# Block 0's later query norm at n = 26 of group 0 instead of n = 6, in a transformer block on Trainium2

## The chip, the cores and the metric

One NeuronCore of a Trainium2 chip. The metric is the device time of one execution in microseconds; the kernel before took 1415.19 us (median of 3 runs, 1414.46 to 1415.21).

## The reference

A pre-norm block in float32 on x of 2048 rows and 512 columns: attention with 32 heads of 16 columns that share one key and one value head, then a gated feed-forward layer with 1792 hidden columns.

```python
q = (layernorm(x) @ wq), 32 heads of 16
k, v = layernorm(x) @ wk, layernorm(x) @ wv
o = softmax(q @ k.T / 4) @ v          # each head against all 2048 keys
h = x + o @ wo
out = h + (gelu(layernorm(h) @ w_gate) * (layernorm(h) @ w_up)) @ w_down
```

## The kernel before, in words

The rows are cut into four blocks of 512 (b = 0 to 3), the heads into eight groups of four. A **prologue** normalizes x, projects the keys and values of all rows, and the queries of block 0. Then comes one long run of **scores**, numbered n. For each block, group and 128 keys (`kc`) there are two scores, n even and odd, of two heads each: two matmuls into a PSUM tile `s`, and one exponential on ScalarE of 128x1024 numbers into `p` (`scores`, line 414). There are three such PSUM tiles, so the score n has to wait until ScalarE has read n - 3. Both n done, `weigh` (line 418) multiplies `p` with the values into `acc`. A group is 32 values of n, a block is 256. What the code calls a pair is one n.

Precision. Queries and keys are split into a high and a low part (`qh`, `ql`), which stand with a bound for the softmax as 50 rows for each head. They go through a DRAM tensor, `q_d`, from which `load_q` fetches a group's 50 rows (`qg`) one group ahead, on the sync engine's queue (SP). Two heads' rows lie at partitions 0 to 49, two at 64 to 113.

**The bound** needs a norm of each query. `project_q` (line 189) projects 128 query columns (8 heads) at a time, c = 0 to 3, from PSUM tiles `pq`, splits them, squares them into `qs`, and its inner function `norm` (line 260) sums the squares by head: one small matmul for each c against the selector `sel` into `pqn` (line 263), a copy to `qn` and its maximum on VectorE (lines 267, 268). `bound`, called two steps of the loop later, works four tiny operations and one of 32x512 on GpSimd (lines 273 to 290) and issues a transfer of the bounds to `q_d` (line 294). `load_q` of a group that the norm covers has to wait for that transfer. Block 0's queries are done as c = 0 alone (`q_first`, groups 0 and 1, in the prologue) and c = 1 to 3 (`q_rest`, groups 2 to 7).

**The queries of blocks 1 to 3** (`later_q`) are projected during block 0's scores, half the rows of PE at a time: one matmul of the projection (line 408, `pq`) runs beside one of the scores (line 410, `s`), on the two halves of the array. `qg_first`, the queries of group 0, therefore holds each head in both halves; the prologue's `first_q` fills one half for each head, `fill_first` (line 346) the other, by two transfers on GpSimd's queue (line 350). The order is set by hand: the loop at n < `lead` takes a string of kinds, "s" a plain score, "m" one beside a projection, from the table `MIXED`; the first mixed one is at n = `START` = 8. From then on `later_q` is asked for its next matmul; where it answers `REST`, a slot of two plain scores is run and behind them what the generator does next: the norm of the block before, at the first c of the next (line 232), or at the end of `later_q`. In that phase `psum1` has one bank, which `pq` and `pqn` use in turn.

At n = 2 the loop takes `q_rest` one step on, which splits c = 3 and writes it to `q_d`, and calls `fill_first`. At n = 6 it takes `q_rest` to its end: the three pqn matmuls for c = 1 to 3 stand on PE behind the score n = 5 and ahead of the first weighing. The generators for blocks 1 to 3 don't run their norm themselves but leave it in the list `norms`.

The order of PE, ScalarE and GpSimd is as the code is recorded throughout, and SP's and VectorE's too in this loop. GpSimd also splits the feed-forward weights during block 0 (`part_weights`: load on SP, cast, difference, store, lines 518 to 533).

Of the kernel before, what the change touches and what calls it, by code (L numbers as in the profile page):

```python
# [13 lines left out]
AF = mybir.ActivationFunctionType  # L14
# [40 lines left out]
def kernel(  # L55
# [12 lines left out]
    nc = tc.nc  # L68
# [83 lines left out]
    def attend(first):  # L152
        with ExitStack() as outer:
            with tc.manual_schedule(
                engines={mybir.EngineType.PE, mybir.EngineType.Pool, mybir.EngineType.Activation}
            ):
                run(outer, first)


    def run(outer, first):  # L160
# [28 lines left out]
        def project_q(b, cs, eng, col, whole=None):  # L189
            halves = whole is not None  # L190
# [3 lines left out]
            urgent = b == 0 and cs[0] == 0  # L194
# [102 lines left out]
                    after.append([2, bound])  # L297
                return qn, mm, m, factors

            if halves:  # L300
                norms.append(norm)
                return
            qn, mm, m, factors = norm()
            if urgent:
                yield 2
                factors()
                nc.scalar.activation(
                    m, qn, AF.Identity, bias=mm[:, 2:3], scale=mm[:, 1:2]
                )
                ms[b] = m  # L310
            else:
                yield 2


        after, squares, norms, pause = [], [], [], [0]
        ms = {}
        q_first = project_q(0, range(FIRST_Q), nc.scalar, 0)
        q_rest = project_q(0, range(FIRST_Q, DC), nc.scalar, NB)

        def later_q():  # L320

            for b in range(1, NB):
                yield from project_q(b, range(DC), nc.vector, b, ())
            yield REST
            yield REST
            norms.pop()()

        def age():
            for entry in after:
                entry[0] -= 1  # L330
            while after and after[0][0] <= 0:
                after.pop(0)[1]()
# [13 lines left out]
        def fill_first():  # L346

            view = q_d.rearrange("h r s -> r h s")
            for a in range(2):
                nc.gpsimd.dma_start(  # L350
                    qg_first[64 * a : 64 * a + KR, 1 - a :: 2, :].bitcast(F32),
                    view[:, 1 - a : 4 : 2, :T].bitcast(F32),
                )
# [71 lines left out]
        def take_out():  # L425
            for step in outs.pop(0):
                step()
# [151 lines left out]
        def load_wo(b):  # L579

            for j in range(DC // 2):
                w = db.tile([P, 2, 2, D], F32R, tag="w2", bufs=W2, name=f"wo_{b}_{j}")
                nc.sync.dma_start(
                    w.bitcast(F32),
                    wo_d[2 * j : 2 * j + 2].rearrange("c p i d -> p c i d").bitcast(F32),
                )
                wos[b, 2 * j], wos[b, 2 * j + 1] = w[:, 0], w[:, 1]
# [416 lines left out]
        def finish(n):  # L1004
            for _ in range(min(n, len(pend))):
                pb, pg, pkc, pp, pacc, _ = pend.pop(0)
                weigh(pacc, pp, pkc)
                if pkc == KC - 1:
                    evacuate(pb, pg, pacc)
# [17 lines left out]
        def score(n, beside=()):  # L1027

            nonlocal acc
            i, u = divmod(n, 2)  # L1030
            b, r = divmod(i, PER)
            g, kc = divmod(r, KC)
            if u == 0:
                if kc == 0:
                    cur["qg"] = qgs.pop((b, g))
                    acc = pss.tile([P, T], F32, tag="acc", bufs=1, name=f"acc_{b}_{g}")
                if kc == 2 and b * NG + g + 1 < NB * NG:
                    key = divmod(b * NG + g + 1, NG)
                    qgs[key] = load_q(*key)
                cur["p"] = sb.tile([P, 4, T], F32, tag="p", bufs=PB, name=f"p_{i}")  # L1040
            scores(i, cur["p"], cur["qg"], kc, u, beside)
            if u == 1:
                pend.append((b, g, kc, cur["p"], acc, n))
# [12 lines left out]
        n, lead = 0, 2 * PER + sum(SIZES[: LEAD[0]])  # L1056
        with tc.manual_schedule(engines={mybir.EngineType.SP, mybir.EngineType.DVE}):
            parts = None
            if first:
                work = later_q()  # L1060
                parts = part_weights(early.enter_context(tc.tile_pool(name="parts", bufs=1)))

            token, left = None, 6 * (NB - 1) * DC * DC
            while n < lead:
                age()
                r = n % (2 * KC) if n >= 2 * KC else n - START if n < 28 else 30
                if first and n == START:
                    token = next(work)
                if (token is None or token == REST and left <= 0) and (n < START or n % 2 == 0):
                    kinds, runs = "ss", 1  # L1070
                elif r < 30:
                    kinds, runs = MIXED[r % 10]
                    if kinds == "ss" and 5 * left > 6 * (LAST_Q - n):
                        kinds = "sm"
                else:
                    kinds, runs = ("mm" if left > LAST_Q - n else "ss"), 1
                rest, held = token == REST, False
                if n == 2 * PER:
                    assert token is None
                    while after:  # L1080
                        age()
                    for _ in parts or ():
                        pass
                    if first:
                        check_bound(eb, k2m)
                    parts = work = None
                    early.close()
                    db = late.enter_context(tc.tile_pool(name="dense", bufs=1))
                    load_wo(0)
                for kind in kinds:  # L1090
                    if kind == "m" and not rest and not held and token not in (None, REST):
                        held = token[1] == 1
                        tokens = token, next(work)
                        score(n, [(lane, step) for lane, _, step in tokens])
                        token = next(work, None)
                        left -= 2
                    else:
                        score(n)
                    n += 1
                if first and n == 2:  # L1100
                    next(q_rest)
                    fill_first()
                if first and n == 6:
                    for _ in q_rest:
                        pass
                if n == 2 * PER + 8:
                    primed = dense(0)
                    next(primed)
                if rest:
                    token = next(work, None)  # L1110
                if len(pend) > 2:
                    finish(runs)
                while squares:
                    squares.pop(0)()
                for _ in range(runs):
                    if outs and not pause[0] and n % (2 * KC) not in (2, 3, 4):
                        take_out()
                    pause[0] = max(pause[0] - 1, 0)
                if parts is not None and n > 12 and n % (2 * KC) % 10 in (0, 6):
                    next(parts, None)  # L1120
            assert n == lead
# [22 lines left out]
        for c in range(LEAD[0], (NB - 1) * NG * len(SIZES)):  # L1144
            b, cb = divmod(c, NG * len(SIZES))
# [316 lines left out]
    def check_bound(sb, k2m):  # L1462
        q2m = sb.tile([H, 1], F32, name="q2m")
        nc.vector.tensor_reduce(q2m, q2, axis=AX.X, op=ALU.max)
        nc.vector.tensor_tensor(q2m, q2m, k2m, op=ALU.mult)
        nc.sync.dma_start(b_d.rearrange("o h -> h o"), q2m)
# [77 lines left out]
```

## Time and profile before

| what | value |
| --- | --- |
| runs | 1414.46, 1415.19, 1415.21 us |
| the profiled execution | 1415.3 us, its span 1413.6 us |
| granted TensorE clock, mean | 0.997 of full |
| TensorE (PE) busy | 1393.2 us, 99% of the span |
| ScalarE (ACT) busy | 1040.9 us, 74% |
| VectorE (DVE) busy | 547.4 us, 39% |
| GpSimd (POOL) busy | 185.0 us, 13% |
| the kernel's scores begin | 51.1 us |

Times are microseconds from the start of the span. A row of a timeline gives start, length, engine, line, operation, what it writes and reads, count, and in brackets how long the engine was idle ahead of it and what ended that. PE overlaps matmuls, so the length of a row is more than its share of PE's time; the distance of starts is the better measure. The chain of waits follows the end back, at each step to what released it.

### The profile page before, as it was taken

What the parts mean: (1) busy time and instruction counts of PE and PEld (TensorE: products, weight loads), DVE (VectorE), ACT (ScalarE), POOL (GpSimd) and SP (SyncE); (2) the same over time, 40 slices, a digit from 0 to 9 for tenths busy, and PEclk for the clock granted to TensorE, in tenths of its full rate; (3) what the DMA queues carried; (4) which work ended last, traced back from release to release, by engine and by line L of the source; (5) the groups of instructions that cost most, each with busy time, mean ns of one, the idle gap of its engine ahead of it and who ended that gap; (6) DMA issues with size and microseconds to landing.
All of it is one profiled execution on the core that took longest, in us unless ns stands there. A gap on an engine that the chain in (4) does not pass through costs nothing.

```text
span 1413.6 us, 25632 instructions
## 1 busy us (share of the span) xinstructions
PE 1393.2 (99%) x10646; PEld 780.2 (55%) x10646; DVE 547.4 (39%) x982; ACT 1040.9 (74%) x1149; POOL 185.0 (13%) x280
## 2 busy tenths in 40 slices
PE   8899999999999999999999999999999999999998
PEld 7433333334555555555555555554555555557886
DVE  7311423323252433434252432414352342427665
ACT  7699999996777777777788777877787777772000
POOL 6445655511000000000000000000000000002000
PEclk9999999999999999999999999999999999999999
DMA  4467788752241332223252332223233241335551
GB/s 159 149 207 253 264 256 250 252 187 83 102 158 64 117 117 87 87 86 142 83 174 72 117 117 87 87 92 115 102 140 107 87 146 49 139 123 201 182 195 59
DMA packets 84840, 194.10 MB, mean 137 GB/s; under 512 B 9776, under 2 KB 24112, under 8 KB 84684
## 3 DMA queue, kind: packets, MB, share of 16 engines
q1 hardware_dynamic: 77572, 167.50, 35.1%
q0 software_dynamic: 6976, 24.78, 4.9%
q8 instruction: 86, 1.41, 0.4%
q14 instruction: 38, 0.31, 0.1%
q10 hardware_dynamic: 168, 0.10, 0.0%
HBM read 142.53 MB, written 49.55 MB: 136 GB/s over the span
## 4 chain that ended last, share of the span: by engine, by line
PE 92%; ACT 3%; DMA 1%; DVE 1%; issue 1%; POOL 1%; SPq 0%; ACTq 0%; DVEq 0%; POOLq 0%
PE acc L418 33%; PE s L410 18%; PE pu L932 8%; PE pg L932 8%; PE pd L932 5%; PE pq L408 4%; PE pd L609 3%; PE pd L631 3%; PE pg L631 3%; PE pu L631 3%; ACT p L414 2%; PE pp L609 2%; PE pp L740 1%; PE pxt L676 1%; DMA x<-in_A_x_dram 0%
## 5 line engine op out<-in xcount | busy, mean ns | idle before, releaser
L414 ACT ACTIVATE p<-s 128x1024 f32<-128x1024 f32 x1024 | 969.5, 1032 | 229.8 <-PE s L410 226.2
L418 PE MATMUL acc<-p,v_sb 128*32 128x512 f32 x4096 | 496.5, 600 | 0.0
L410 PE MATMUL s<-qg,kaug 50*128 50x512 f32 x1984 | 416.4, 424 | 3.6 <-ACT p L414 3.5
L410 PEld LDWEIGHTS s<-qg,kaug 50*128 50x128 f32 x1984 | 193.5, 184 | 219.7 <-ACT p L414 122.3
L418 PEld LDWEIGHTS acc<-p,v_sb 128*32 128x32 f32 x4096 | 109.6, 109 | 230.8 <-issue 227.4
L932 PE MATMUL pu<-x2h,w 64*128 64x512 f32 x672 | 212.2, 391 | 0.0
L932 PE MATMUL pg<-x2h,w 64*128 64x512 f32 x672 | 211.3, 391 | 0.1
L932 PEld LDWEIGHTS pu<-x2h,w 64*128 64x128 f32 x672 | 115.9, 185 | 15.0
L932 PEld LDWEIGHTS pg<-x2h,w 64*128 64x128 f32 x672 | 116.0, 185 | 14.6 <-DVE g L806 0.6
L932 PE MATMUL pg<-x2l,w 64*128 64x512 f32 x336 | 122.0, 390 | 0.0
L932 PE MATMUL pu<-x2l,w 64*128 64x512 f32 x336 | 122.0, 390 | 0.0
L809 ACT ACTIVATE ga<-ga 128x512 f32<-128x512 f32 x56 | 35.3, 634 | 89.2 <-DVE ga L804 89.2
L131 POOL TENSOR_SCALAR rstd<-mv 128x1 f32<-128x1 f32 x16 | 3.6, 223 | 683.4 <-DVE mv L129 683.3
L932 PE MATMUL pd<-w,gh 64*128 64x512 f32 x384 | 81.2, 392 | 0.0
L874 DVE TENSOR_TENSOR h<-h,pd 128x512 f32<-128x512 f32 x48 | 31.9, 685 | 115.4 <-PE pd L932 66.3
L1171 DVE SCALAR_TENSOR_TENSOR ga<-ga,g 128x512 f32<-128x512 f32 x70 | 48.4, 691 | 51.9 <-ACT ga L809 50.9
L458 DVE RECIPROCAL oc<-oc 128x128 f32<-128x128 f32 x64 | 56.6, 923 | 28.9 <-DMA oc<-acc_d 24.1
L793 DVE COPY g<-pg 128x512 f32<-128x512 f32 x56 | 38.8, 692 | 63.2 <-PE pg L932 57.5
L932 PEld LDWEIGHTS pu<-x2l,w 64*128 64x128 f32 x336 | 58.0, 185 | 7.1
L932 PEld LDWEIGHTS pg<-x2l,w 64*128 64x128 f32 x336 | 58.0, 185 | 7.0
L431 DVE COPY oT<-acc 128x512 f32<-128x512 f32 x32 | 22.1, 692 | 96.9 <-PE acc L418 94.5
L806 DVE SCALAR_TENSOR_TENSOR g<-g,pu 128x512 f32<-128x512 f32 x56 | 38.2, 683 | 40.7 <-PE pu L932 30.4
(245 smaller groups left out, 1453.5 us busy)
## 6 DMA issues: line engine op xcount, KB each, us to landing
w<-w_d SPq DMA_DIRECT2D x112, 512.0 KB
w<-w_d SPq DMA_DIRECT2D x28, 1024.0 KB
qg<-q_d SPq DMA_DIRECT2D x48, 200.0 KB
q_d<-qh SPq DMA_DIRECT2D x32, 256.0 KB
wo<-wo_d SPq DMA_DIRECT2D x8, 1024.0 KB
acc_d<-oT SPq DMA_DIRECT2D x31, 256.0 KB
oc<-acc_d SPq DMA_DIRECT2D x124, 64.0 KB
w_d<-w_0b POOLq DMA_DIRECT2D x14, 512.0 KB, 6.6
```

The costliest lines, as they stand in the source:

```text
L408: step()
L410: nc.tensor.matmul(s[:, a, :], kaug[rows, kc * P : (kc + 1) * P], qg[rows, 2 * u + a, :], start=True, stop=True,)
L414: nc.scalar.activation(p[:, 2 * u : 2 * u + 2, :], s, AF.Exp, scale=SCALE)
L418: nc.tensor.matmul(acc[32 * j : 32 * j + 32, :], v_sb[:, kc, :], p[:, j, :], start=(kc == 0), stop=(kc == KC - 1), skip_group_check=True,)
L458: nc.vector.reciprocal(oc[:, 1, sl], oc[:, 1, sl])
L609: nc.tensor.matmul(banks[k], lhsT[rows], rhs[rows], start=(turn == 0 and i == 0), stop=(turn == 1 and i == n - 1), skip_group_check=True,)
L631: nc.tensor.matmul(bank, lhsT, rhs, start=(i == 0), stop=(i == len(ts) - 1))
L793: nc.vector.tensor_copy(g, pg)
L806: nc.vector.scalar_tensor_tensor(g, g, 0.5, pu, op0=ALU.mult, op1=ALU.mult)
L809: nc.scalar.activation(a, a, AF.Tanh, scale=GELU_A * GELU_C)
L932: nc.tensor.matmul(e["bank"], lhsT[rows], rhs[rows], start=i == 0 and not e["both"], stop=last and e["both"], skip_group_check=True,)
L1171: (soon or lazy).pop(0)()
```

## The change

`project_q` no longer runs the norm of a call that is not urgent: it leaves it in `norms`, for `q_rest` as for blocks 1 to 3. The loop takes `q_rest` to its end at n = 2. The next to look into `norms` is block 1's first c, at its `REST`, so the norm of block 0's later queries runs there. This is a REST that there was none of before, at n = 26 and 27, and the mixed scores behind it move down by one slot.

```diff
@@ project_q, at its end
-            if halves:
+            if not urgent:
                 norms.append(norm)
                 return
             qn, mm, m, factors = norm()
-            if urgent:
-                yield 2
-                factors()
-                nc.scalar.activation(
-                    m, qn, AF.Identity, bias=mm[:, 2:3], scale=mm[:, 1:2]
-                )
-                ms[b] = m
-            else:
-                yield 2
+            yield 2
+            factors()
+            nc.scalar.activation(
+                m, qn, AF.Identity, bias=mm[:, 2:3], scale=mm[:, 1:2]
+            )
+            ms[b] = m
@@ the loop over n
                 if first and n == 2:
-                    next(q_rest)
-                    fill_first()
-                if first and n == 6:
                     for _ in q_rest:
                         pass
+                    fill_first()
```

What stands on PE behind the score n = 5 (`s_1_841`), before the change, with the semaphores that an instruction waits for; DVE, Activation and Pool are VectorE's, ScalarE's and GpSimd's, DMASW0 and DMASW1 those of the first and the second transfer on GpSimd's queue, which are the two of `fill_first`:

```order
L410 MATMUL s_1_841<-qg_first,kaug 128x512
L263 LDWEIGHTS sel
L263 MATMUL pqn_1_845<-qs_1_722,sel 32x512
L263 LDWEIGHTS sel
L263 MATMUL pqn_1_845<-qs_2_765,sel 32x512 [waits DVE_49]
L263 LDWEIGHTS sel
L263 MATMUL pqn_1_845<-qs_3_817,sel 32x512 [waits DVE_49]
L418 MATMUL acc_0_803<-p_804,v_sb 32x512 [waits DMAHW5_49,DMAHW4_49]
L418 MATMUL acc_0_803<-p_804,v_sb 32x512 x3
L410 MATMUL s_0_859<-qg_first,kaug 128x512 [waits Activation_49]
```

And after it, on to the first score that runs beside a projection, n = 8 (`s_0_864`):

```order
L407 MATMUL s_1_841<-qg_first,kaug 128x512
L415 MATMUL acc_0_803<-p_804,v_sb 32x512 [waits DMAHW5_49,DMAHW4_49]
L415 MATMUL acc_0_803<-p_804,v_sb 32x512 x3
L407 MATMUL s_0_850<-qg_first,kaug 128x512 [waits Activation_49]
L407 MATMUL s_0_850<-qg_first,kaug 128x512
L407 MATMUL s_1_854<-qg_first,kaug 128x512 [waits Activation_49]
L407 MATMUL s_1_854<-qg_first,kaug 128x512
L415 MATMUL acc_0_803<-p_824,v_sb 32x512 x4
L405 MATMUL pq_0_862<-xT_hi_85,wq_hi 128x512
L407 MATMUL s_0_864<-qg_first,kaug 128x512 [waits DMASW1_49,Activation_49,Pool_49]
```

The three pqn matmuls are gone from there; the score n = 8 waits for the same semaphores as before. (The two waits on DMAHW in the weighing are for loads of the prologue.)

On PE at n = 26 (`s_0_1024`) and 27 after the change, where before a score and a projection of block 1's second c stood side by side:

```order
L407 MATMUL s_0_1024<-qg_first,kaug 128x512
L407 MATMUL s_1_1028<-qg_first,kaug 128x512 [waits Activation_49]
L407 MATMUL s_1_1028<-qg_first,kaug 128x512
L263 LDWEIGHTS sel
L263 MATMUL pqn_1_1032<-qs_1_722,sel 32x512 [waits DVE_49]
L263 LDWEIGHTS sel
L263 MATMUL pqn_1_1032<-qs_2_765,sel 32x512
L263 LDWEIGHTS sel
L263 MATMUL pqn_1_1032<-qs_3_817,sel 32x512
L415 MATMUL acc_0_803<-p_983,v_sb 32x512 x4
L405 MATMUL pq_1_1049<-xT_hi_85,wq_hi 128x512 [waits DVE_49]
```

The first pqn waits for VectorE's copy out of `pq_0`, the next projection for the copy out of `pqn`. From n = 34 on PE's order is the same as before, to the end of the program. On GpSimd the norm's five operations and its transfer move from ahead of the first weight's cast (`wo0`) to ahead of the third weight's store; on SP the load `wo3r` now stands ahead of the writes of block 1's first `qh` and `ql`; on VectorE the copy to `qn` and the maximum move from ahead of block 1's first `mark` to behind its `pq_raw`.

## The prediction

> **What bounds the kernel now.** I read the page's busy shares and its chain first, then the chain around the edit, then single engines there. The page, busy time by engine and the chain by engine:
>
> ```profile
> PE 1393.2 (99%) x10646; PEld 780.2 (55%) x10646; DVE 547.4 (39%) x982; ACT 1040.9 (74%) x1149; POOL 185.0 (13%) x280
> ...
> PE 92%; ACT 3%; DMA 1%; DVE 1%; issue 1%; POOL 1%; SPq 0%; ACTq 0%; DVEq 0%; POOLq 0%
> ```
>
> TensorE (PE) sets the end almost everywhere: a microsecond of PE time lost or won counts in full, unless something else then holds PE. The chain from 50 to 68 us (start, length, what), where the norm stands now:
>
> ```profile
> 50.25 5.96 DMA q_d<-qh
> 56.33 0.44 DVE qh L121
> ...
> 58.14 0.59 PE pqn L263
> 58.72 1.71 PE acc L418 x8
> ...
> 67.90 1.00 PE acc L418 x8
> ```
>
> The reader is to see two things. The norm's third matmul (pqn) waits for `qs_3`, which waits for a `qh` buffer that a transfer frees at 56.2. And what PE does after that is slow: eight acc matmuls take 1.71 us there, 1.00 us at 67.90. ScalarE's exponentials (start, length, last field the idle time ahead):
>
> ```profile
> 51.79 5.61 ACT L414 ACTIVATE p<-s 128x1024 f32<-128x1024 f32 x6 [0.71 <-PE s L410]
> 61.20 1.94 ACT L414 ACTIVATE p<-s 128x1024 f32<-128x1024 f32 x2 [3.80 <-PE s L410]
> 64.03 20.94 ACT L414 ACTIVATE p<-s 128x1024 f32<-128x1024 f32 x22 [0.90 <-PE s L410]
> ```
>
> Six scores, a hole of 3.80 us, two scores, a hole of 0.90 us, then no hole for 22. The change goes at the first hole. What matters is when the score at n = 8, the first that runs beside a projection, can start. PE there:
>
> ```profile
> 55.13 0.61 PE L263 MATMUL pqn<-qs,sel 128*32 128x512 bf16 x2
> 58.14 0.59 PE L263 MATMUL pqn<-qs,sel 128*32 128x512 bf16 x1 [2.40 <-DVE qs L248]
> ...
> 63.23 0.50 PE L408 MATMUL pq<-xT_hi,wq_hi 64*128 64x512 f32 x1
> 63.29 0.47 PE L410 MATMUL s<-qg_first,kaug 50*128 50x512 f32 x1
> ...
> 68.83 0.49 PE L408 MATMUL pq<-xT_hi,wq_lo 64*128 64x512 f32 x1
> 68.83 0.49 PE L410 MATMUL s<-qg_first,kaug 50*128 50x512 f32 x1
> ```
>
> **What the change removes, and what is late next.** Gone from n = 6 are three pqn matmuls and the 2.40 us that PE sat behind the third. Without them the first weighing starts at 55.13 and takes 1.00 us, to 56.13. The scores n = 6 and 7 need ScalarE to have read n = 3 and 4: at 5.61/6 = 0.935 us each that is at 55.53 and 56.47, so they end by about 56.8; the second weighing ends at 57.8. PE stands before n = 8 at 57.8, not at 63.23, 5.4 us sooner.
>
> But the score n = 8 also waits for the second of the two transfers that fill the other halves of `qg_first` (DMASW1 in the order shown with the change). They are issued by GpSimd. The tile's rows, first for the first issue alone, then for both (durations of the issue, starts; below, issue to landing as least, median, most):
>
> ```profile
> L350 POOL DMA_DIRECT2D qg_first<-q_d x1: 921/921/921, 54.2 to 54.2; - x1
> ...
> DMA to landing us min/median/max: 6.9/6.9/6.9
> ```
>
> ```profile
> L350 POOL DMA_DIRECT2D qg_first<-q_d x2: 696/808/921, 54.2 to 55.1; - x2
> ...
> DMA to landing us min/median/max: 6.9/7.5/8.1
> ```
>
> So the first lands at 54.2 + 6.9 = 61.1, and the second, issued at 55.1, took 8.1 and lands at 63.2. That is just when n = 8 starts today: its score follows its projection by 0.06 us (63.23, 63.29), where the pair at 68.83 starts both together. PE and the transfer arrive at the same moment now. The change leaves the two issues in their place on GpSimd's queue, behind the same correction of the keys, and no transfer between 50 and 63 us moves (the norm's own 48 KB is issued at 63.02). So n = 8 still starts at 63.2: the stall moves from the norm to the fill. **Gain: 0** (at most the 5.4 us, if the fill were not late). The scores n = 6 and 7 run 3.8 us earlier, and ScalarE then idles from 59.3 (57.40 + 2 x 0.935) instead.
>
> **The clock.** The granted clock in four short stretches, each with its length and the busy time of five engines:
>
> ```profile
> 56.15:56.20 0.05, 0.00 (x0) 0.00 (x0) 0.00 (x0) 0.05 (x1) 0.00 (x0) 0.97 0.63 246
> 56.20:56.25 0.05, 0.00 (x0) 0.00 (x0) 0.00 (x0) 0.05 (x1) 0.00 (x0) 0.50 0.73 287
> 63.00:63.05 0.05, 0.05 (x4) 0.00 (x0) 0.00 (x0) 0.05 (x1) 0.03 (x1) 0.76 0.64 246
> 1411.20:1411.30 0.10, 0.00 (x0) 0.00 (x0) 0.00 (x0) 0.00 (x0) 0.00 (x0) 0.94 0.00 0
> ```
>
> The last three numbers are the clock, the share of the DMA engines and GB/s. The clock fell to half at 56.20 and came back at 63.02, 4.88 us after PE took up work at 58.14. Today that slow stretch ends just before 63.23 and so costs nothing, since the fill is awaited anyway. After the change PE stands still from about 58.0 to 63.2, 5.2 us, and its slow stretch begins where the dense work does. At the slow clock eight acc matmuls take 1.71 against 1.00, a factor of 1.71, so each slow microsecond loses 1 - 1/1.71 = 0.42. From n = 8 on ScalarE has no slack to lend: 20.94/22 = 0.952 us a score against 0.935 undisturbed, and the chain from 58.14 to 100 us is PE's, so the loss stays.
>
> How long is it slow? The bounds: nothing, if the clock holds through the gap, and 6.82 us (56.20 to 63.02), the longest slow stretch of the trace, which loses 2.9. The row as it stands, 4.88 us, loses 2.05. The trace lets me see a bit more. The last change, a fall at about 1411.29, lies 1348.27 us after 63.02, and 1348.27/395 = 3.413 is also half of 6.82: as if the clock were decided every 3.41 us, on what PE did since the last decision. Then the restart at 58.14 was slow for 1.47 us up to 59.61 and one whole step more. A restart at 63.2 would, with this run's steps, be warm at 66.43: 3.2 us, a loss of 1.35. Where the steps lie in another run I can't tell; between the two rows I take 3.6 us: **+1.5 us**.
>
> [...]
>
> **What it adds.** The three pqn matmuls go to a slot at n = 26 to 28, in the stretch where PE has no slack. The later blocks' norms stand in just such slots. The chain at the last of them (four matmuls there):
>
> ```profile
> 289.40 0.75 PE pqn L263 x3
> 290.15 1.07 PE acc L418 x6
> 291.23 0.67 PE s L410 x4
> ```
>
> From 289.40 to 291.23 is 1.83 us for four pqn and one weighing, 0.83 more than the 1.00 of a weighing alone (67.90, above): 0.21 each, and **+0.6 us** for three. They need no new wait: `qs_3` is ready since 58.1. Bounds: 0, if the slot had slack, and 0.9, if `pq_1` has to wait for the one PSUM bank that it now shares with pqn in turn. The mixed slots themselves only move down by one; a plain slot at the end of the group becomes mixed. The work is the same.
>
> **Off PE.** On VectorE the copy and the maximum (2 x 0.68 us) go between `pq_raw` and `qh` of block 1; VectorE has holes of several microseconds there, and block 1's scores, which need that `qh`, begin only at n = 256. On GpSimd the five small operations and the transfer stand ahead of the third store of `wo`; that queue next waits for `wo3r` anyway, whose load SP now issues sooner. SP's load of group 2 has to wait for the norm's transfer:
>
> ```profile
> 60.26 0.26 POOL L273 TENSOR_SCALAR mm<-q,k2m 32x1 f32<-32x1 f32 x1 [4.46 <-DVE q L268]
> ...
> 63.02 0.61 POOL L294 DMA_DIRECT2D q_d<-m  x1 [0.29 <-POOL m L290]
> ...
> 90.74 0.77 SPq L390 DMA_DIRECT2D qg<-q_d  x2
> ```
>
> With pqn done near 84.5, the maximum at 86, 63.02 - 60.26 = 2.8 us on GpSimd and about 8 us for the transfer (as for the fills), it lands near 97, 6 us after that load is due. Group 2 begins at n = 64, about 51.8 + 64 x 0.952 + 4.7 (the two holes) = 117, so the load has 20 us left. Cost 0; it would begin to cost if the transfer or the load took over 10 us longer.
>
> **Sum.** 0 + 1.5 + 0.6 = +2.1 us. The profiled execution took 1415.3 (span 1413.6, and 1.7 around it), 0.1 above the median of 1415.19: **1417.4 us**, 0.15% more. About 0.2%, 2.8 us, is what a measurement of this kernel can tell from no change.
>
> **Rivals.**
>
> *The stall really goes.* If the fill is not what holds n = 8, the score starts at 57.8: -5.4 + 0.6 = -4.8, 1410.5. For it: the biggest hole of ScalarE is 3.80 us and its named cause is removed. Against: 55.1 + 8.1, and the 0.06 us. A milder form: the second transfer lands when the first does, at 61.1: -2.1 + 0.6, and 0 to 1.5 for the clock, 1413.8 to 1415.3.
>
> *The clock holds.* Then only the matmuls are paid: +0.6, 1415.9. Against: today 2.40 us of standing still, after a sparse stretch, were enough for a fall.
>
> *A long slow stretch, slower beyond the bound.* The same mechanism at n = 8, with the restart falling so that PE is slow for two whole steps: 6.82 x 0.42 = 2.9, and with the bank's wait 0.6 to 0.9 more, 1418.8 to 1419.1. It decides from (2.8 - 0.6)/0.42 = 5.3 us of half clock on. For it: 4.88 was seen already.
>
> *The change does nothing.* The order shows the pqn matmuls gone from n = 6, so this could only be by the fill's wait, which is my forecast without its losses.
>
> **How the numbers follow.** Forecast 0.66, the clock holds 0.10, the long stretch 0.13, the milder early fill 0.05, the stall gone 0.06. The range takes all but the last: 1413.8 to 1419.2. Slower than the bound: the long stretch and the upper end of my own case, 0.25; faster: the stall gone and a little of the mild form, 0.07; within: 0.68.
>
> **What would show it.** In the profile after: PE idle before the s matmul of n = 8, from about 58 to 63, released by the fill (or by nothing that the view names); ScalarE's hole behind the eighth exponential, some 4.5 us, not behind the sixth; a granted clock of 0.5 behind 63 us, and acc groups of 1.7 us there; a pqn group near 84 us. I am wrong if n = 8 starts before 61, or if the clock is full at 63.5.

## The result and the profile after

| kernel | median, us | runs, us |
| --- | --- | --- |
| before, in this series | 1415.19 | five, 1414.46 to 1415.53 |
| after | 1421.87 | 1418.31, 1420.57, 1421.87, 1422.96, 1425.93 |

The ratio is 1.0048, 95% interval [1.0027, 1.0069]: slower, by 6.7 us at the median where +2.1 was forecast, and above the range's end of 1419.2. The profiled execution after is the fastest of the five, 1418.3 us with a span of 1416.5. That one differs by 3.0 us from the profile before, and its rows follow the forecast step by step. The rest of the loss, 3.6 us to the median, isn't in it at all; the experiments look for it.

The page of the kernel after, busy time by engine and the chain by engine:

```profile
PE 1396.1 (99%) x10646; PEld 784.7 (55%) x10646; DVE 549.2 (39%) x982; ACT 1041.1 (74%) x1149; POOL 186.6 (13%) x280
...
PE 91%; ACT 3%; DVE 2%; DMA 2%; POOL 1%; issue 1%; SPq 0%; ACTq 0%; DVEq 0%; POOLq 0%
```

PE still sets the end. It does the same 10646 matmuls and is busy 2.9 us longer, so the time went into slower matmuls rather than more of them. The chain around the change, start, length, what:

```profile
55.04 7.86 DMA qg_first<-q_d
63.04 0.76 PE s L407
...
65.51 3.54 PE acc L415 x16
...
83.56 0.54 PE pqn L263 x2
84.10 1.07 PE acc L415 x6
85.17 0.42 PE pq L405
```

The first score beside a projection (63.04) is released by the second transfer of the fill, issued at 55.04 and 7.86 us under way. Sixteen weighings behind it take 3.54 us, 1.77 for eight. The norm now stands at 83.56: three pqn and a weighing take 1.61 us to 85.17. PE and then ScalarE there, with the idle time and its end in brackets:

```profile
59.29 0.50 PE L405 MATMUL pq<-xT_hi,wq_hi 64*128 64x512 f32 x1
63.04 0.76 PE L407 MATMUL s<-qg_first,kaug 50*128 50x512 f32 x1 [3.25 <-DMA qg_first<-q_d]
```

```profile
51.74 5.61 ACT L411 ACTIVATE p<-s 128x1024 f32<-128x1024 f32 x6 [0.70 <-PE s L407]
57.69 1.94 ACT L411 ACTIVATE p<-s 128x1024 f32<-128x1024 f32 x2 [0.34 <-PE s L407]
64.27 2.85 ACT L411 ACTIVATE p<-s 128x1024 f32<-128x1024 f32 x3 [4.64 <-PE s L407]
```

ScalarE's hole behind the sixth exponential is down from 3.80 to 0.34 us; a hole of 4.64 us stands behind the eighth. The edges of the granted clock (the third number from the right is the clock):

```profile
58.60:58.65 0.05, 0.05 (x4) 0.00 (x0) 0.00 (x0) 0.05 (x2) 0.00 (x0) 0.56 0.72 287
62.05:62.10 0.05, 0.00 (x0) 0.00 (x0) 0.00 (x0) 0.00 (x0) 0.00 (x0) 0.57 0.84 328
68.85:68.90 0.05, 0.05 (x4) 0.00 (x0) 0.00 (x0) 0.00 (x0) 0.00 (x0) 0.66 0.42 82
```

It comes back to full at 58.64, falls at 62.06 while PE waits, and returns at 68.88, so 5.84 us of the work restarted at 63.04 run at half clock.

### The profile page after: what moved, and what is told of

Read it like the earlier page. It is cut to its first block, busy times and chain, and to the rows that moved or that the text cites. A ratio compares the mean times of both kernels' runs of the same rounds, so it can differ in the third digit from the quotient of the medians.

```text
span 1416.5 us, 25632 instructions
## 1 busy us (share of the span) xinstructions
PE 1396.1 (99%) x10646; PEld 784.7 (55%) x10646; DVE 549.2 (39%) x982; ACT 1041.1 (74%) x1149; POOL 186.6 (13%) x280
## 4 chain that ended last, share of the span: by engine, by line
PE 91%; ACT 3%; DVE 2%; DMA 2%; POOL 1%; issue 1%; SPq 0%; ACTq 0%; DVEq 0%; POOLq 0%
PE acc L415 33%; PE s L407 18%; PE pu L929 9%; PE pg L929 8%; PE pd L929 4%; PE pq L405 4%; PE pd L606 3%; PE pd L628 3%; PE pg L628 3%; PE pu L628 3%; ACT p L411 2%; PE pp L606 2%; PE pp L737 1%; DMA acc_d<-oT 1%; DMA qg_first<-q_d 1%
```

## The experiments

The yardstick in every trace is the start of VectorE's copy of a finished group's sums out of PSUM, `oT`: how much later it comes than in the profile before shows where time is lost. Group 0 ends at about 90 us, group 7, the last of block 0, at 304, group 8 at 339.

**The changed kernel again, with PE kept busy, and with an early fill.** Four kernels: the changed one unchanged; the changed one with 18 projection matmuls of 128x512 whose sum nobody reads, ahead of the score n = 8, to keep the clock up through the wait:

```diff
                 if first and n == START:
+                    idle = psum1("idle")
+                    for _ in range(18):
+                        nc.tensor.matmul(
+                            idle, wq_hi[:, 0, :P], xT[1][0][:, 0, :], start=True, stop=True
+                        )
                     token = next(work)
```

and the second fill of `qg_first` issued earlier, in the prologue, in the changed kernel and in the kernel before:

```diff
-                for b in range(1, NB):
+                low_k(1, vTs[1])
+                fill_first(qg)
+                for b in range(2, NB):
                     low_k(b, vTs[b])
...
-                    fill_first()
```

> The changed kernel once more, for more times and a second trace. Clock theory (the score n = 8 is held by the fill of qg_first until 63 us, PE's clock falls meanwhile and stays at half for a number of 3.41 us steps that differs from run to run): ratio to before 1.001 to 1.008 with a spread of several us again, a trace with the score n = 8 at 63 us, and a mean granted clock that is the lower the longer the run. Rival (the extra time is the norm in its new slot and the bound's late transfer): the same time in every run to within 1 us, the clock the same.

> The changed kernel with 18 projection matmuls of 512 columns, whose result nobody reads, on PE ahead of the first mixed score (18 x 0.23 = 4.1 us, inside the wait for the fill from 59 to 63 us). Clock theory: full clock behind 63 us, the spread of the runs below 1.5 us, and about 0.6 us over before (the norm's matmuls alone): 1415.5 to 1416.5. Rival: nothing changes against the changed kernel, 1418 to 1426.

> The changed kernel with the two fills of qg_first issued on GpSimd's queue behind the key corrections of block 1, ahead of those of blocks 2 and 3 (5.6 us earlier, but not before the bounds of group 0 are in, about 50.5 us). Clock theory: the second fill lands at about 59, the score n = 8 starts at 58 to 59, ScalarE's hole of 4.6 us is nearly gone, and the time is 1410 to 1412, 3 to 5 us below before. Rival: the fill isn't what holds n = 8; the time stays that of the changed kernel.

> The kernel before with the same earlier fills. Both theories: PE stands behind the third matmul of the norm until 58.1 whatever the fill does, and reaches n = 8 at 63.2 at half clock: 1414.5 to 1415.5, no change. If it gains 2 us or more, PE was waiting for the fill in the kernel before, too.

| kernel | median, us | range, us | ratio to before, 95% |
| --- | --- | --- | --- |
| after again (7 runs) | 1421.08 | 1416.7 to 1424.7 | 1.0043 [1.0028, 1.0058] |
| after, PE busy (12) | 1419.55 | 1417.3 to 1424.2 | 1.0022 [1.0006, 1.0038] |
| after, early fill (12) | 1412.82 | 1411.7 to 1418.7 | 0.9975 [0.9961, 0.9989] |
| before, early fill (12) | 1416.71 | 1415.7 to 1422.9 | 1.0009 [0.9995, 1.0022] |

The kernel before, on this chip, had a median of 1416.67 (30 runs, 1414.6 to 1423.8): it too has executions well above its usual time. The early fill does nothing for the kernel before and takes 8.3 us off the changed one, whose wait at n = 8 goes with it. So the fill is what the changed kernel waits for there; 8.3 us is more than the 2.0 to 3.8 us by which group 0 comes sooner there than in the two traces of the changed kernel, so part of it lies elsewhere. PE with the added matmuls, then ScalarE:

```profile
59.32 4.37 PE L1067 MATMUL idle<-xT_hi,wq_hi 128*128 128x512 f32 x18
63.85 0.47 PE L407 MATMUL s<-qg_first,kaug 50*128 50x512 f32 x1
```

```profile
64.58 19.10 ACT L411 ACTIVATE p<-s 128x1024 f32<-128x1024 f32 x20 [5.32 <-PE s L407]
```

PE starts the score at 63.85, 0.56 us later than the 63.29 of before, and no slow matmul follows: the granted clock is 1.00 from 60 to 72 us, and 20 exponentials have no hole. Group 0 comes 1.17 us late: 0.56 and 0.61 for the norm's matmuls. In the profile after, the start is 0.25 us sooner than before, 5.84 us at half clock lose 0.42 each, 2.45, and the norm 0.61: together +2.8, against +3.12 measured at group 0. So the terms of the clock and of the norm are real, the norm's as large as put and the clock's, in this execution, larger (2.45 for 1.5).

But the medians are far above that (1419.55 with PE kept busy, where 1415.5 to 1416.5 was expected, and a spread of 7 us for 1.5), and group 0 explains none of the rest. One trace did show a second place: the kernel before with the early fill, profiled at 1420.3, is 1.60 us late at group 7 and 5.30 at group 8. The next four kernels go there.

**The load of `wo`.** Ahead of the first projection of the output, SP issues the load of `wo` (`load_wo`) and behind it block 0's last turn of the sums through memory (`acc_d<-oT`, then `oc<-acc_d`). The load goes to memory of the pool `early`, and so waits until the last transfers out of that pool have landed: the last norm's bounds, tile `m`, from GpSimd, and a check's tile `q2m`, from SP. A pool with the split weights is closed at the same point; the store of the last of them, `w213b`, also on GpSimd's queue, is a third such transfer, as SP's waits show further down. First `m` alone was put into the pool that lives to the end, in both kernels and in the one with the early fill; and the kernel before got 18 small subtractions on GpSimd at the place where the changed one has the norm:

```diff
-                m = eb.tile([H, T], F32R, tag="m", bufs=2, name=f"m_{b}_{cs[0]}")
+                m = const.tile([H, T], F32R, tag="m", bufs=2, name=f"m_{b}_{cs[0]}")
```

```diff
                 age()
+                if first and n == 30:
+                    hold = eb.tile([P, P], F32, name="hold")
+                    for _ in range(18):
+                        nc.gpsimd.tensor_tensor(hold, ident, ident, op=ALU.subtract)
```

> The kernel before, with the tile m of every norm's bound taken from the pool that lives to the end instead of from the pool `early` that is closed at 300 us, so that the load of wo (304 us) no longer waits for the last bound's transfer; nothing else moves. Theory A (the time that the change lost beyond its place near 63 us arises at 300 to 328 us: a late weight chain on GpSimd makes the last bound late, the load of wo waits for its transfer, runs into block 0's last turn of the output, and TensorE waits and goes to half clock in the first projection): the slow executions of the kernel before (its median in the last series 1416.7, about half of its runs above 1416) go, median 1414.0 to 1415.5. Rival B (wo's load waits for something else of the pool as well, or the collision on the queues stays): no change, 1416 to 1417.

> The changed kernel with the same edit: the tile m of the norms in the pool that lives to the end. Theory A: what is left of the loss is the place near 63 us alone, oT copies +1.2 to +3.1 us against before, median 1416.0 to 1418.0, and the shift against before is the same at group 7 and at group 8. Rival B: no change, 1420 to 1422, with a step of some 3 us between group 7 and group 8 in the slower executions.

> The kernel before, with 18 subtractions of 128x128 on GpSimd between the split of the third row of wo and its store, where the changed kernel has the moved norm (there GpSimd was held from 81.9 to 89.7 us, 3.9 of it waiting). Theory A1 (the norm's new place makes the chain of weight splits late, and so the last bound, and so the load of wo, in most executions): median up by 2 to 4 us, to 1418 to 1421, with the oT copies unchanged up to group 7 and later from group 8 on. Rival A2 (the chain follows the DMA's landings and makes up for 8 us of work; its lateness is chance): the distribution of before, median 1416 to 1417.

> Both remedies in the changed kernel: the second fill of the first queries issued in the prologue (1412.8 without the second remedy) and the tile m in the pool that lives to the end. Theory A: the two losses are separate and both go, median 1410.5 to 1412.0. Rival B: as without the second remedy, 1412.5 to 1413.5.

| kernel | median, us | range, us | ratio to before, 95% |
| --- | --- | --- | --- |
| before, `m` kept (12 runs) | 1416.38 | 1415.0 to 1422.1 | 1.0003 [0.9988, 1.0018] |
| after, `m` kept (11) | 1418.84 | 1416.2 to 1420.0 | 1.0011 [0.9998, 1.0023] |
| before, GpSimd held (12) | 1415.72 | 1414.5 to 1422.2 | 0.9998 [0.9982, 1.0014] |
| after, early fill, `m` kept (12) | 1414.34 | 1411.7 to 1421.9 | 0.9992 [0.9974, 1.0009] |

In these series the kernel before had a median of 1416.25 (35 runs, 1414.6 to 1423.0). Theory A held for the changed kernel in that its executions above 1420 us are gone, though the median is 0.8 us above the range given. It failed for the kernel before, which kept such executions (1422.1), and with the early fill neither theory held: 1414.34, four of 12 above 1417. Theory A1 failed: holding GpSimd costs nothing. There the load went out at 302.29, 1.27 us ahead of the copy, and the step from group 7 to group 8 is 0.5 us.

**Four more traces of the changed kernel**, one execution each, to see one above 1420 us. (A window of half clock, in the expectations, is one of the steps of 3.41 us.)

> The changed kernel as it is, for one more trace: its times reach from 1416.7 to 1425.9 us and the two traces so far are of its fastest executions (1418.3 and 1416.7). Theory A: an execution above 1420 us shows, beyond the +1.3 to +3.3 us of the place at 63 us (oT copies of group 0 against before), a step of 2 to 4 us between group 7 and group 8, with the load of wo waiting for the last bound's transfer and TensorE at half clock in the first projection. Rival B: the step lies at 63 us itself (a fill that lands later or a third window of half clock; group 0 at +5 or more). Rival C: several small steps further on, after group 8.

> A further trace of the changed kernel; the same expectations as for the first of these: above 1420 us theory A has the step between group 7 and group 8, rival B has it in group 0, rival C after group 8; at or below 1419 us only the shift of group 0 stands (+1.3 to +3.3).

> A further trace of the changed kernel; the same expectations as for the first of these: above 1420 us theory A has the step between group 7 and group 8, rival B has it in group 0, rival C after group 8; at or below 1419 us only the shift of group 0 stands (+1.3 to +3.3).

> A further trace of the changed kernel; the same expectations as for the first of these: above 1420 us theory A has the step between group 7 and group 8, rival B has it in group 0, rival C after group 8; at or below 1419 us only the shift of group 0 stands (+1.3 to +3.3).

How much later than in the profile before `oT` comes, in us, in every trace with the norm at n = 26, the late fill and no added matmuls; the last two are kernels with kept tiles:

| trace | time | group 0 | group 7 | group 8 | last group |
| --- | --- | --- | --- | --- | --- |
| after | 1418.3 | +3.12 | +3.05 | +3.33 | +2.96 |
| after again | 1416.7 | +1.31 | +1.27 | +1.32 | +1.38 |
| trace a | 1423.1 | +2.15 | +2.09 | +7.55 | +7.62 |
| trace b | 1418.2 | +2.12 | +2.07 | +2.69 | +2.84 |
| trace c | 1419.5 | +2.44 | +2.44 | +4.26 | +4.13 |
| trace d | 1423.2 | +2.19 | +2.13 | +8.25 | +7.83 |
| after, `m` kept | 1418.8 | +3.30 | +3.22 | +3.22 | +3.48 |
| after, both kept | 1416.3 | +0.84 | +0.85 | +1.01 | +0.76 |

That settles where it is in these two: both executions above 1420 us have a second step of 5.5 and 6.1 us between group 7 and group 8, larger than the 2 to 4 expected, and nothing of that size elsewhere. Rivals B and C are out for them. VectorE's copies for groups 7 and 8, first before, then trace d:

```profile
303.56 0.69 DVE L431 COPY oT<-acc 128x512 f32<-128x512 f32 x1 [11.34 <-PE acc L418]
...
339.04 0.69 DVE L431 COPY oT<-acc 128x512 f32<-128x512 f32 x1 [1.33 <-PE acc L418]
```

```profile
305.69 0.69 DVE L428 COPY oT<-acc 128x512 f32<-128x512 f32 x1 [11.34 <-PE acc L415]
...
347.29 0.69 DVE L428 COPY oT<-acc 128x512 f32<-128x512 f32 x1 [1.33 <-PE acc L415]
```

SP's own queue between them, before and trace d:

```profile
300.01 0.90 SPq L583 DMA_DIRECT2D wo<-wo_d  x2
304.28 0.34 SPq L435 DMA_DIRECT2D acc_d<-oT  x1
```

```profile
299.75 1.53 SPq L1461 DMA_DIRECT2D b_d<-q2m  x1
307.15 1.71 SPq L580 DMA_DIRECT2D wo<-wo_d  x2
308.91 0.73 SPq L432 DMA_DIRECT2D acc_d<-oT  x1
```

Before, the load is out 3.55 us ahead of the copy. In trace d it waits until 307.15, and the turn, whose copy ended at 306.4, stands behind it in SP's order until 308.91. The chain of trace d:

```profile
300.88 5.89 DMA q_d<-m
...
308.91 8.50 DMA acc_d<-oT
...
321.14 3.40 DVE oc L455 x4
...
325.77 1.22 PE pp L606 x4
...
328.28 4.66 PE acc L415 x32
```

The bounds' transfer lets the load go, the load's 2 MB run beside the turn (8.50 us from issue to landing, 6.84 in trace a and 7.25 in the profile after; in the profile before SP goes on to `oc` 5.11 us behind the issue, 309.39 - 304.28), and the reciprocals, the high part of the output and the projection (pp) follow late. PE, then the clock:

```profile
325.77 1.22 PE L606 MATMUL pp<-wo,o_hi 64*128 64x512 f32 x4 [4.23 <-DVE o_hi L466]
```

```profile
323.50:323.60 0.10, 0.00 (x0) 1.00 0.80 307
325.50:325.60 0.10, 0.00 (x0) 0.50 1.10 451
328.50:328.60 0.10, 0.10 (x4) 0.50 0.70 287
```

PE waits 4.23 us for `o_hi`, and restarts at half clock: the 32 weighings take 4.66 us instead of the 3.57 of the profile before. It is the same pair, a wait and then a slow restart, as at 63 us.

**Both tiles kept.** With `m` alone kept the load still stood at 302.1 and 304.3. What SP waited for in the changed kernel ahead of the load, with `m` kept (us in total, times, longest):

```profile
SPq L580 <- DMA w_d<-w213b: 4.1, 1, 4.1
SPq L580 <- DMA b_d<-q2m: 0.4, 1, 0.4
```

In the kernel before with `m` kept it was 3.3 and 0.7. So `q2m` has the last word, but most of the wait is for the store of `w213b`. What was kept next is `q2m`:

```diff
-        q2m = sb.tile([H, 1], F32, name="q2m")
+        q2m = const.tile([H, 1], F32, name="q2m")
```

> The kernel before with both late readers, the tiles m and q2m, in the pool that lives to the end, so that the load of wo waits for neither transfer. Theory A (the load of wo, let go late, runs into the last turn of block 0's output and so makes TensorE wait at 317 to 327 us): the load is issued before 299 us and the executions above 1418 us go; median 1414.5 to 1416, highest below 1419. Rival B (the step between group 7 and 8 has another cause, such as the transfers of the queries on the same queue): the distribution stays, with a quarter of the runs above 1419 us.

> The changed kernel with both tiles in the pool that lives to the end. Theory A: only the place near 63 us is left, +1.3 to +3.3 us against the kernel before; median 1416.5 to 1418.5, none above 1420. Rival B: some runs at 1421 to 1425, with a step between group 7 and 8.

> The changed kernel with the early second fill and both tiles kept. Theory A: neither place costs anything; median 1411 to 1413, none above 1416. Rival B: as with the tile m alone, median 1413 to 1415 with single runs up to 1422.

| kernel | median, us | range, us | ratio to before, 95% |
| --- | --- | --- | --- |
| before, both kept (12 runs) | 1415.89 | 1414.8 to 1417.4 | 0.9999 [0.9989, 1.0008] |
| after, both kept (12) | 1418.51 | 1416.3 to 1424.8 | 1.0020 [1.0008, 1.0031] |
| after, early fill, both kept (12) | 1414.86 | 1412.6 to 1418.6 | 0.9996 [0.9983, 1.0008] |

SP in the kernel before with both kept:

```profile
298.83 0.90 SPq L583 DMA_DIRECT2D wo<-wo_d  x2
304.59 0.34 SPq L435 DMA_DIRECT2D acc_d<-oT  x1
```

The load goes out 5 us ahead of the copy, as theory A said, and none of 12 executions is above 1418 us. That alone shows little: in the same series 3 of 29 runs of the kernel before were above 1418, in all series 28 of 112. In the changed kernel one of 12 is above 1420 (1424.8, of which there is no trace), where none was expected; its load in the profiled execution went out only at 302.87, and SP's wait ahead of it says why:

```profile
SPq L580 <- DMA w_d<-w213b: 4.7, 1, 4.7
```

With both tiles kept the load still waits, for the last weight's store. No run kept that tile as well, so the wait was shortened and never removed. With the early fill as well the median, 1414.86, and six of 12 runs above 1416 miss theory A (1411 to 1413). Changed against before, both with both tiles kept, is 1418.51 - 1415.89 = 2.6 us: about the price of the place at 63 us. The lead of the load over the copy of group 7, beside the step between group 7 and group 8, in all traces:

| trace | load ahead of copy, us | step, us |
| --- | --- | --- |
| before, both kept; before | 5.04; 3.55 | -0.1; 0 |
| after, `m` kept; after; before, `m` kept | 2.44; 1.87; 1.83 | 0; 0.3; 0.2 |
| after again; after, both kept; trace b | 1.67; 1.54; 1.35 | 0.1; 0.2; 0.6 |
| before, GpSimd held; after, PE busy | 1.27; 1.02 | 0.5; 0.3 |
| after, early fill, six traces in order of the lead | 4.30; 3.00; 2.40; 2.31; 1.61; 1.02 | 0.2; 0.1; 0.9; 0.2; 0.6; 0.9 |
| trace c | 0.18 | 1.8 |
| before, early fill | -0.12 | 3.7 |
| trace d; trace a | -1.46; -2.38 | 6.1; 5.5 |

More than 1 us ahead it costs at most 0.9; less, in four traces, 1.8 to 6.1.

**The early fill once more.** The three kernels with it gave 1412.8, 1414.3 and 1414.9, only the first measurably below the kernel before. The first was timed again, and the one with both tiles kept traced twice more.

> The changed kernel with the early second fill once more, timed as in its first series (1412.8, ratio 0.9975). Theory A (the stall at the first mixed score goes from the norm to the fill, and with the fill early it goes altogether): again below the kernel before, median 1412 to 1414, ratio 0.997 to 0.999. Rival B (the first series had luck; without the stall the rest still costs what was gained): median 1414 to 1416, ratio 0.999 to 1.000.

> The changed kernel with the early fill and both tiles kept, for a trace. If it runs above 1416 us: theory A has the extra 3 to 5 us between group 7 and group 8 (group 0 at -2 to -3 us against before, group 8 at +1 or more); rival B has it in group 0 (TensorE at half clock around 60 us for one or two more windows, group 0 at 0 to +2 us); rival C later. Below 1414 us: group 0 and group 8 both at -2 to -3 us.

> The same kernel for a further trace, with the same expectations: above 1416 us theory A has the extra time between group 7 and group 8, rival B in group 0, rival C later; below 1414 us neither.

The repeat gave 1415.30 (12 runs, 1411.4 to 1420.9), ratio 0.9995 [0.9980, 1.0009], the two traces 1413.97 and 1412.48 us. In the second trace group 0 is 3.46 us sooner than before. ScalarE there, and the fill's rows:

```profile
57.79 1.94 ACT L411 ACTIVATE p<-s 128x1024 f32<-128x1024 f32 x2 [0.47 <-PE s L407]
59.97 19.09 ACT L411 ACTIVATE p<-s 128x1024 f32<-128x1024 f32 x20 [0.24 <-PE s L407]
```

```profile
L347 POOL DMA_DIRECT2D qg_first<-q_d x2: 693/807/921, 50.5 to 51.5; - x2
...
DMA to landing us min/median/max: 7.0/7.0/7.0
```

The second transfer lands at 58.5, and both holes of ScalarE are gone. So what the change aims at is there to be had: group 0 is 0.7 to 3.5 us sooner in the six traces of the changed kernel with the early fill. How much sooner goes with the clock: it was at half for one step of 3.41 us in the trace at -3.46 (54.94 to 58.36) and for three in the one at -0.67 (53.80 to 64.04). At 0.42 lost per us a step costs 1.43, so the four between, at -2.0 to -2.6, would fit two steps, an estimate from these two. What of it is left at the end is small: the four medians lie 3.9, 1.9, 0.8 and 1.3 us below the kernel before in the same series, and only the first difference is more than its interval. No trace caught one of the longer executions (five of the repeat's 12 are above 1416), so where those lose their time is open. The repeat lies in the range of rival B: the gain of the first series did not hold up.

## Why the prediction was wrong

*The stall moves to the fill, gain 0: right.* The score n = 8 started at 63.04 (61.97 to 63.25 in the eight traces of the table), released by the fill, in the row where it was forecast; the early fill removed the wait and the kernel before gained nothing by it.

*The clock, +1.5: right in kind, near in size.* In the profile after the clock fell while PE waited, and eight weighings took 1.77 us; it was slow for 5.84 us, 2.45 lost. In the eight traces the slow stretch behind n = 8 was 3.4 us in five and 4.6, 5.8 and 6.1 in the others, 4.2 on average where 3.6 was put, and with PE kept busy there was none. In these five it began only 0.1 to 1.4 us behind the restart: an edge that came after the wait still dropped the clock. How long went with where the edges lay, as the prediction said: one step of 3.41 us where the fall came behind the restart, 4.6 to 6.1 us where the clock was at half already. Its count of 395 steps supports the 3.41 less than it looks, since 394 or 396 would give 3.42 and 3.40; the edges of twelve traces do (last section). That the clock is decided on what PE did since the last edge was the author's estimate, and the runs bear it out only in part. In the profile after, PE was busy 34% of the step ahead of the fall at 62.06 and all of the one ahead of the return at 68.88; but in the profile before it was busy 60% of the step ahead of the fall at 56.20, and 60% of the one before that, behind which the clock stayed full.

*Three pqn, +0.6: right.* 1.61 - 1.00 = 0.61.

*The sum of these, +2.1: right for what it covered.* The eight traces have group 0 at +0.84 to +3.30, 2.2 on average; that the mean is so close is in part luck, as single executions are over 1 us off either way. The difference of the medians with the second place eased in both kernels is 2.6.

**The step that failed is "Off PE ... Cost 0", and with it the sum's carrying +2.1 unchanged to the end.** It followed SP to the load of group 2 and VectorE to block 1's `qh`, and stopped there. The load of `wo`, 200 us on, is an order of two instructions on SP, and whether it costs anything is decided by which of two chains is later: GpSimd's chain of weights, with the last weight's store and the last bounds, or block 0's scores. The one profiled execution of the kernel before had the load out 3.55 us ahead there and none of its first five runs was over 1415.6, so nothing in that page's largest rows pointed to it; but the load's wait and the turn behind it stood in SP's timeline. Of 112 further executions of the kernel before 16 were above 1420 us, of the changed kernel 11 of 16, with `m` kept 0 of 11 and with both kept 1 of 12. In the three traces above 1420 us (a, d, and the kernel before with the early fill) the step at that place is 3.7 to 6.1 us, and with its wait shortened the changed kernel's median is 1418.5 to 1418.8 instead of 1421 to 1422.

Why the changed kernel loses that race so much more often is not settled. The last weight's cast on GpSimd starts at 292.0 to 296.0 us in its six traces, and in five of kernels with the norm in its old place at 284.6, 288.0, 291.1, 291.8 and 293.9. It is later by a few microseconds, but so is the copy, by 2. Holding GpSimd for 9.4 us where the norm holds it for 7.8, at the same place, gave 291.8 and no loss in the median, so the hold alone isn't it.

Of the rivals, the long slow stretch is what the profile after shows at 63 us (5.84 us, above its point of 5.3). It, too, ended at 1419.1 and did not have the second place; that the profiled execution, at 1418.3, lies in the forecast's range says nothing for the range, as it is the fastest of the five.

## What to carry to other kernels

Ask of a wait that is removed which semaphores the next instruction still has: here a transfer landed within 0.1 us of the old stall's end, and moving that transfer was the real change. A profile of one execution prices the races as they came out in it: list the places where an issue in a fixed order waits for another engine's chain (here a load into a pool's freed memory), note how many microseconds they are won by, and price a shift against those margins. Tiles that are read last by slow transfers don't belong in a pool whose end something on the critical path awaits; which transfers these are is read from the waits ahead of the load (here two tiles were moved, and a third still held it for 4.7 us).

## What the runs showed of the hardware that I had not expected

The clock's edges lay 3.41 us or a multiple of it from each other, to 0.02 us, in each of twelve traces between 50 and 72 us (before, after, after again, a to d, the changed kernel with `m` kept, with both kept, with PE busy and with the early fill, and the second trace with the early fill and both kept), but the first fall lay anywhere from 53.1 to 56.2 us. A step of full work at half clock was not always enough to bring it back. In the changed kernel with the early fill, three steps at half clock and the edge behind them (length, busy time of PE, clock):

```profile
53.80:57.20 3.40, 3.28 (x12) 0.50 0.64 195
57.21:60.61 3.40, 3.40 (x18) 0.50 0.53 199
60.63:64.02 3.39, 3.39 (x18) 0.50 0.57 206
64.05:64.10 0.05, 0.05 (x4) 1.00 0.32 125
```

PE was busy 96% of the first, all of the second and all of the third, and was at half clock for 10.2 us. The second trace of the changed kernel had 89% and then a full step, and was back behind that:

```profile
53.50:56.87 3.37, 3.00 (x12) 0.50 0.54 171
56.87:60.27 3.40, 3.40 (x16) 0.50 0.62 206
60.30:63.68 3.38, 1.86 (x18) 1.00 0.55 201
```

Here the clock returned behind the first full step, above only behind the second. What makes the difference, the runs don't tell. The longest stretch, in trace c from 53.9 to 67.6 us, was four steps, with PE busy 93%, 100%, 43% and 100%. The fill's time from issue to landing, for 200 KB on GpSimd's queue, was 6.6 to 8.1 us in fifteen traces, so the moment that n = 8 waits for moves by more than a microsecond from one execution to the next.
